# Pooled attention and a SiLU layer: one more seven-product unit in two tiles, weight sums one tile earlier, and two PSUM banks swapped

## The chip, the cores and the metric

The kernel runs on one core of a Trainium2 chip. The metric is the device time of one execution in microseconds; lower is better. Before the change three runs gave 282.60, 282.61 and 282.72 us, the median is 282.61.

## What is computed

Two stages in a row. The first is attention with keys and values that are averaged over groups of 8 positions (8 batches, 8 heads, 576 positions, 64 elements a head, so 72 pooled keys). The second multiplies the 4608 resulting rows of 512 by `w_in` (512 x 2048), applies SiLU, and multiplies by `w_out` (2048 x 512).

```python
k_p = k.reshape(B, H, Sp, pool, D).mean(axis=3)
v_p = v.reshape(B, H, Sp, pool, D).mean(axis=3)
scores = scale * np.matmul(q, k_p.transpose(0, 1, 3, 2))
attn = np.exp(scores - np.max(scores, axis=-1, keepdims=True))
attn = attn / (np.sum(attn, axis=-1, keepdims=True) + 1e-09)
x = np.matmul(attn, v_p)            # then transposed to rows of 8 * 64
h = x @ w_in
g = h * (1.0 / (1.0 + np.exp(-h)))
out = g @ w_out
```

## The kernel before

**Tiles.** The 4608 rows are taken in nine tiles of 512 (the loop over `t` at L793). Each tile has a first product (`up`, L460: `x` times `w_in`, SiLU into `h_T`) and a second product (`down` L562 in tile 0, `down_quarters` L632 in the others). The attention of batch `t + 1` is worked into the steps of tile `t`. Its results go into `xT`, a ring that holds the rows of four batches.

**Order.** Nothing is scheduled by the compiler: each engine runs its instructions in the order in which the Python code emits them. `spread` (L406) mixes two streams. A step of the product is two or four matmuls of `up`, or one of `down`; before it goes on past step `i`, it emits every "filler" that is due at `i` or earlier. `f_up` and `f_down` are the lists of fillers of a tile's two products, pairs of a due step and a function. So the due step sets the place in each engine's queue, and it sets nothing else: an instruction on DVE starts when the ones ahead of it on DVE are done and its own data are there.

**Units.** The 2048 columns of `w_in` are 16 groups of 128. A plain group (`plain`, L527) is four matmuls of 512 columns. Four groups can be computed as a "unit" (`UNITS` L417: groups 4 to 7, 8 to 11, 12 to 15): a two-by-two block scheme with seven products in place of eight (the Winograd form of Strassen's scheme). Its products are numbered 2, 5, 1, 4, 3, 7, 6 (`stage`, L491); each is four matmuls of 256 columns into one of three PSUM banks P, Q and R (L477). ScalarE copies P (`r_sb`, L494), DVE forms `rr_sb` (L497), `t_sb` (L500) and two sums `c_sb` (L509, L512), and ScalarE takes SiLU of P, Q and of the two sums (L485, the letters `h` and `s`). A unit needs five sums of parts of `x` (`unit_x_sum`, L442) and five sums of parts of `w_in` (`unit_weight_sum`, L435). In the lists at L807 to L821, `G(12)` is a plain group, `(0, "251")` are three products of unit 0; in `THREE` (L786) the letters A, B, C name units 0, 1, 2 (`"BCA".index` maps them to numbers), `g` a plain group. Before the change tile 1 has one unit and twelve plain groups, tile 2 two units and eight, tiles 3 to 8 three units and four.

**The second product.** From tile 1 on it uses the same scheme with seven products over sums of `h_T` (`hidden_sum`, L602) and five sums of quarters of `w_out` (`weight_sum`, L620). Each of these is emitted in four DVE instructions of 128 x 512. In `W_SUMS` (L612), `W11` and `W12` are rows 0 to 7 (of 16 groups of rows) of the left and right half of `w_out`, `W21` and `W22` rows 8 to 15. Sums 1 and 3 are emitted in tile 0's second product (steps 48 and 52), sums 4, 7 and 6 in tile 1's first product (steps 38, 42 and 60), at L834.

**Loads around it.** All loads from L706 on stand in POOL's queue in the order of the code. `w_out` comes in four quarters of four row groups (`load_w_out`, L729): quarters 0, 1 and 2 (L775), then three loads of the values of batch 1 (L777 to L779), then quarter 3 (L780). In tile 0's second product DVE pools these values (`slot_sums("v", j)`, due at steps 20 and 30, L849), PE selects the pooled rows (`select_v`, L294, steps 37 and 40), DVE copies them (`copy_v`, L308), and the attention of batch 1 is finished (`numerators`, L371, steps 44, 55 and 56), whose DVE products (L393) write the `xT` that tile 1 reads.

**Banks.** PSUM's eight banks are two rings: "mm" with three banks, "at" with five (L89). A new tile takes the oldest bank of its ring, and its first writer waits until the last reader of that bank is done. In the prologue (L736 to L769) `numerators(0, part(1, 0), ("mm", "at"))` puts its first product in an "mm" bank and its second in an "at" bank; the scores that follow take four "at" banks.

Of the kernel before, what the change touches and what calls it, by code (L numbers as in the profile page):

```python
# [36 lines left out]
def kernel(  # L37
# [11 lines left out]
    B, H, S, D = q.shape  # L49
# [148 lines left out]
    def pool_k(b):  # L198
        pool_rows(kp[:SP], batches[b]["k_raw"])
# [91 lines left out]
    def copy_k(b, a, copy=nc.vector.tensor_copy):  # L291
        copy(out=kz[b % 2][:, a], in_=batches[b]["kz_ps"][:, a])
# [21 lines left out]
    def part(g, f):  # L314
        return ((g, f * QF, (f + 1) * QF),)
# [302 lines left out]
    PW = 4  # L618
# [73 lines left out]
    def warm_up(n):  # L692
        for _ in range(n):
            nc.tensor.matmul(warm_ps, lhsT=warm[:, :128], rhs=warm, start=True, stop=True)  # L694
# [70 lines left out]
    scores(0, part(0, 1))  # L765
    q_transpose(0, 1, 1)
    warm_up(1)
    numerators(0, part(1, 0), ("mm", "at"))
    scores(0, part(1, 1))  # L769
    load_slots(nc.gpsimd, 1, "k", 0, 3)  # L770
    load_slots(nc.gpsimd, 1, "k", 3, 4)
# [21 lines left out]
    for t in range(NT):  # L793
        a = t + 1
        f_up, f_down = [], []
        if t == 0:
            GA = 11
            items = [(g, 0, HS) for g in range(GA)]
            items += [(g, HS, NTT - HS) for g in range(GA)]
            items += [(g, 0, NTT) for g in range(GA, KG)]  # L800
            f_up += [(1, lambda: denominators(0, part(0, 1), on_dve=True))]
            f_up += [(5, lambda: denominators(0, part(1, 1), on_dve=True))]
            f_up += [(13, lambda: numerators(0, part(0, 1)))]
            f_up += [(17, lambda: numerators(0, part(1, 1)))]
        else:
            G = lambda *gs: [(g, 0, NTT) for g in gs]
            if t == 1:  # L807
                items = (
                    G(12, 13, 14, 15) + [(0, "251")] + G(8) + [(0, "43")] + G(9)
                    + [(0, "7h6")] + G(10) + [(0, "s")] + G(11, 0, 1, 2, 3)  # L810
                )
            elif t > 2:
                items = []
                for it in THREE[t // B].split():
                    items += [(("BCA".index(it[0])), it[1])] if it[0] in "ABC" else G(int(it[1]))
            else:
                items = (
                    G(12, 13) + [(0, "251")] + G(14) + [(0, "43")] + G(15) + [(0, "76")]
                    + [(1, "2")] + [(0, "hs")] + [(1, "51")] + G(0) + [(1, "43")] + G(1)
                    + [(1, "7h6")] + G(2) + [(1, "s")] + G(3)  # L820
                )  # L821
            if t < 3:
                for n in U_X:
                    f_up.append((0, lambda n=n: unit_x_sum(t, n)))
            for n in (2, 5):
                h_at = 50 if t == B else 54 if t > 2 else 45
                f_up.append((h_at, lambda n=n: hidden_sum(n, 4, 8)))
            f_up.append((56, lambda: hidden_sum(6, 4, 8)))
            for n, k0 in ((2, 0), (5, 0), (1, 4), (1, 0)):
                f_up.append((64, lambda n=n, k0=k0: hidden_sum(n, k0, k0 + 4)))  # L830
            f_down.append((33, lambda: hidden_sum(7, 0, 8)))
            f_down.append((71 if t < B else 50, lambda: hidden_sum(6, 0, 4)))

        for n, t0, f_to, at, parts in (  # L834
            (1, 0, f_down, 48, (0, PW)), (3, 0, f_down, 52, (0, PW)),
            (4, 1, f_up, 38, (0, PW)), (7, 1, f_up, 42, (0, PW)),
            (6, 1, f_up, 60, (0, PW)),
        ):
            for i in range(*parts):
                if t == t0:  # L840
                    f_to.append((at + i, lambda n=n, i=i: weight_sum(n, i)))
        if a < B:
            q_at = [4, 14, 4, 8] if t > 2 else [15, 16, 17, 8] if t > 1 else [24, 25, 26, 2] if t else [82, 84, 86, 88]
            if t == 0:
                for j in range(2):
                    f_up.append((44 + 8 * j, lambda j=j: slot_sums("k", j)))
                    f_up.append((72 + 8 * j, lambda j=j: select_k(1, j)))
                    f_up.append((72 + 8 * j, lambda j=j: copy_k(1, j)))
                    f_down.append((20 + 10 * j, lambda j=j: slot_sums("v", j)))  # L849
                    f_down.append((37 + 3 * j, lambda j=j: select_v(1, j, "at")))  # L850
                    f_down.append((37 + 3 * j, lambda j=j: copy_v(1, j)))
            elif t == 1:
                for j in range(2):
                    f_up.append((0, lambda j=j: slot_sums("k", j, halves=True)))
                    f_up.append((22, lambda j=j: select_k(2, j)))
                    f_up.append((23, lambda j=j: copy_k(2, j)))
                    f_down.append((8, lambda j=j: slot_sums("v", j, halves=True)))
                    f_down.append((40, lambda j=j: select_v(2, j, "at")))
                    f_down.append((41, lambda j=j: copy_v(2, j)))
            else:  # L860
                f_up.append((1, behind_x_sums))
                f_up.append((1, lambda: pool_k(a)))
                if a + 1 < B:
                    f_up.append((2, lambda: load_one(a + 1, "k")))
                f_up.append((2, lambda: pool_v(a)))
                f_up.append((40, lambda: k_transpose(a)))
            for n in range(4):
                f_to = f_down if t and n >= (2 if t > 2 else 3) else f_up
                f_to.append((q_at[n], lambda n=n: q_transpose(a, n % 2, n // 2)))
            if t == 0:  # L870
                f_down.append((0, lambda: load_half_2("k", 0)))
                f_down.append((0, lambda: load_q(2)))
                f_down.append((0, lambda: load_half_2("k", 1)))
                for half in range(2):
                    f_down.append((31, lambda half=half: load_half_2("v", half)))
                for y in range(2):
                    for n in U_W:
                        f_down.append((6, lambda y=y, n=n: unit_weight_sum(y, n)))
            elif a + 1 < B:
                if t == 1:  # L880
                    f_up.append((0, lambda: load_one(a + 1, "k")))
                f_to, at = (f_up, 4) if t > 1 else (f_down, 11)
                f_up.append((5 if a + 1 == B - 1 else 0, lambda: load_q(a + 1)))
                f_to.append((at, lambda: load_one(a + 1, "v")))
                f_up.append((5, lambda: load_rest(a + 1, "k")))
                f_to.append((at + 2, lambda: load_rest(a + 1, "v")))
            f_down.append((0, attn_tables))

            if t:
                sc_at, den_at, nu_at = (1, 31, 75), (31, 56, 97), (56, 97, 101)  # L890
            else:
                sc_at, den_at, nu_at = (1, 16, 30), (16, 30, 44), (44, 55, 56)
            for n, sg in enumerate(visits):
                f_down.append((den_at[n], lambda sg=sg: denominators(a, sg)))
                f_down.append((sc_at[n], lambda sg=sg: scores(a, sg)))

            for n, sg in enumerate(visits):
                if n < 2 or not 0 < t < B - 2:
                    f_down.append((nu_at[n], lambda sg=sg: numerators(a, sg)))
                if n == 0 and 1 < t < B - 1:  # L900
                    f_down.append((nu_at[n], lambda: numerators(a - 1, visits[2])))
        if 1 < t < B:
            for n in (4, 1, 3, 7, 6):
                f_down.append((98 if t < B - 1 else 44, lambda n=n: unit_x_sum(t + 1, n)))
        if t == 1:
            def unit_weight_tiles():
                k_w = big.tile([128, 4, 2, 256], BF16, tag="k_raw2", name="w_sum12")
                v_w = big.tile([128, 4, 2, 256], BF16, tag="v_raw2", name="w_sum12")
                w_sum1.append([k_w[:, i] for i in range(4)] + [v_w[:, 0]])

            f_down.append((72, unit_weight_tiles))
            for i, n in enumerate(U_W):
                f_down.append((73 if i < 2 else 81, lambda n=n: unit_weight_sum(2, n)))
        moe_tables()
        up(t, f_up, items)
        if t == 0:
            down(t, f_down, [(0, 1, 2), (3,)])
        else:
            down_quarters(t, f_down, last=t == NT - 1)
# [28 lines left out]
```

The softmax here doesn't subtract the row's maximum and nothing guards it: scores larger than these inputs give would overflow.

## Time and profile before

| | us |
|---|---|
| median of three runs | 282.61 |
| the profiled execution | 282.59 |
| its span in the profile | 280.5 |
| busy PE / DVE / ACT / POOL | 275.4 / 218.2 / 187.7 / 98.7 |
| tile 0's second product begins | 32.84 |
| tile 1, 2, 3, 4 begin | 51.11, 81.35, 111.62, 140.35 |
| tile 1's, tile 2's second product begins | 65.18, 94.50 |

The span is the time from the first to the last instruction; the execution's own time has 2.09 us around it. All times of single instructions are microseconds from the span's start. In a timeline a line gives the start, the time until the last of the group ends, engine, source line, operation, what is written from what, and how many; in square brackets stand the idle time ahead of it and what ended it. PE is TensorE, PEld its weight loads, DVE VectorE, ACT ScalarE, POOL GpSimd, SP SyncE. The profile's ends of matmuls are modelled, so starts are what is compared here.

### The profile page before, as it was taken

Reading aid. Unit: us, or ns where it says so; the run is one execution under the profiler, and the core shown is the slowest. Engines: PE = TensorE matmul, PEld = TensorE weight load, DVE = VectorE, ACT = ScalarE, POOL = GpSimd, SP = SyncE. Lnnn points to the kernel's source line nnn. Section 1 sums busy time; section 2 is a strip of 40 time slices with the busy share of each in tenths; the row PEclk is TensorE's granted clock in tenths of the full one; section 3 lists DMA queues with packets and bytes.
Section 4 is the critical chain, followed back from the end, with each engine's and each line's share of the span. In section 5 each row is a group of like instructions: output and inputs, shape, how many; then the busy total and the mean of one; then the engine's idle time right before and its main releaser. Section 6 shows DMA issues by size and latency. Waiting matters only on the chain.

```text
span 280.5 us, 7088 instructions
## 1 busy us (share of the span) xinstructions
PE 275.4 (98%) x2853; PEld 201.4 (72%) x2853; DVE 218.2 (78%) x409; ACT 187.7 (67%) x365; POOL 98.7 (35%) x104
## 2 busy tenths in 40 slices
PE   8999999999999999999999999999999999999995
PEld 4448444556777578867888878787877778788684
DVE  4886746889887876897689768885888588966983
ACT  1688765668677776797579857984799578326700
POOL 8745217332138630863077106970640000000001
PEclk9999999999999999999999999999999999999999
DMA  7999999795659769569755944699610041004104
GB/s 210 284 260 238 210 325 171 227 197 94 148 72 203 200 108 170 129 181 132 138 132 154 135 65 121 141 144 139 160 26 2 0 105 49 0 11 109 33 4 148
DMA packets 31312, 37.70 MB, mean 134 GB/s; under 512 B 10352, under 2 KB 22256, under 8 KB 31280
## 3 DMA queue, kind: packets, MB, share of 16 engines
q0 software_dynamic: 23920, 27.03, 51.7%
q1 hardware_dynamic: 6928, 9.58, 12.4%
q10 hardware_dynamic: 432, 0.66, 0.6%
q8 instruction: 22, 0.36, 0.5%
q14 instruction: 10, 0.08, 0.1%
HBM read 36.70 MB, written 9.44 MB: 164 GB/s over the span
## 4 chain that ended last, share of the span: by engine, by line
PE 82%; DMA 12%; DVE 3%; issue 1%; ACT 1%; DVEq 0%
PE o_psP L645 15%; PE o_psQ L645 15%; PE hp_ps L537 13%; PE u_psP L477 10%; PE u_psQ L477 10%; PE o_psR L645 5%; DMA w_out_sb<-in_moe_w_out_dram 5%; DMA raw<-in_k_dram 4%; DMA q_bf<-in_q_dram 3%; PE u_psR L477 3%; PE sc_ps L340 3%; PE nu_ps L384 2%; PE warm_ps L694 2%; PE den_ps L358 2%; PE warm_ps L698 1%
## 5 line engine op out<-in xcount | busy, mean ns | idle before, releaser
L645 PEld LDWEIGHTS <-h_sum 128*128 128x128 bf16 x640 | 60.4, 98 | 13.1 <-DVE h_sum L605 2.7
L537 PE MATMUL hp_ps<-xT,w_in_sb 128*128 128x512 bf16 (+3 forms) x300 | 58.1, 337 | 0.1
L605 DVE TENSOR_TENSOR h_sum<-h_T 128x1024 bf16<-128x1024 bf16 (+1 forms) x72 | 51.9, 771 | 1.0 <-ACT h_T L543 1.0
L477 PEld LDWEIGHTS <-w_sum 128*128 128x128 bf16 x420 | 41.1, 98 | 7.7
L543 ACT ACTIVATE h_T<-hp_ps 128x512 bf16<-128x512 f32 (+2 forms) x71 | 36.3, 528 | 12.9 <-PE hp_ps L537 11.7
L348 ACT ACTIVATE es<-sc_ps 72x384 bf16<-72x384 f32 (+1 forms) x100 | 39.1, 470 | 8.8 <-PE sc_ps L340 8.7
L537 PEld LDWEIGHTS <-w_in_sb 128*128 128x128 bf16 x300 | 28.6, 98 | 18.4 <-issue 1.1
L485 ACT ACTIVATE h_T<-c_sb 128x512 bf16<-128x512 f32 x42 | 26.1, 627 | 4.9 <-DVE c_sb L509 4.3
L393 DVE TENSOR_TENSOR xT<-nu_ps,rec 128x384 bf16<-128x384 f32 (+1 forms) x50 | 24.0, 532 | 4.3 <-PE nu_ps L384 4.3
L645 PEld LDWEIGHTS <-h_T 128*128 128x128 bf16 x256 | 24.1, 98 | 4.5 <-issue 0.9
L549 POOL DMA_DIRECT2D out_dram<-o_sb x2 | 1.2, 618 | 68.3 <-issue 67.6
L367 ACT ACTIVATE lnd<-den_ps 128x384 f32<-128x384 f32 (+1 forms) x23 | 11.1, 484 | 19.7 <-PE den_ps L358 19.7
L190 POOL TENSOR_TENSOR raw<-raw 72x1024 f32<-72x1024 f32 x10 | 23.6, 2360 | 0.1
L500 DVE TENSOR_TENSOR t_sb<-u_psR,rr_sb 128x512 f32<-128x512 f32 x21 | 14.5, 692 | 6.7 <-PE u_psR L477 4.8
L494 ACT COPY r_sb<-u_psP 128x512 f32<-128x512 f32 x21 | 12.3, 584 | 10.1 <-PE u_psP L477 8.7
L263 DVE TENSOR_TENSOR raw<-raw 128x384 f32<-128x384 f32 (+3 forms) x20 | 12.4, 618 | 8.5 <-DMA raw<-in_v_dram 4.9
L645 PE MATMUL o_psP<-w_out_sb,h_sum 128*128 128x256 bf16 x128 | 17.7, 273 | 0.6 <-DVE h_sum L605 0.6
L477 PEld LDWEIGHTS <-w_in_sb 128*128 128x128 bf16 x168 | 16.1, 98 | 2.6
L497 DVE TENSOR_TENSOR rr_sb<-u_psQ,r_sb 128x512 f32<-128x512 f32 x21 | 14.3, 681 | 3.7 <-ACT r_sb L494 2.1
L509 DVE TENSOR_TENSOR c_sb<-u_psP,t_sb 128x512 f32<-128x512 f32 x21 | 14.4, 687 | 3.1 <-ACT h_T L485 1.4
L196 POOL COPY gate<-x_sum 1x1 bf16<-1x1 bf16 x5 | 0.9, 180 | 44.9 <-DVE x_sum L444 44.9
L645 PE MATMUL o_psQ<-w_sum,h_sum 128*128 128x256 bf16 x128 | 16.7, 273 | 0.0
(84 smaller groups left out, 518.6 us busy)
## 6 DMA issues: line engine op xcount, KB each, us to landing
out_dram<-o_sb SPq DMA_DIRECT2D x128, 64.0 KB, 1.8
raw<-in_k_dram POOLq DMA_DIRECT2D x10, 576.0 KB, 8.1
raw<-in_v_dram POOLq DMA_DIRECT2D x10, 576.0 KB, 7.8
q_bf<-in_q_dram POOLq DMA_DIRECT2D x6, 576.0 KB, 10.9
w_in_sb<-in_moe_w_in_dram POOLq DMA_DIRECT2D x8, 256.0 KB, 8.5
w_out_sb<-in_moe_w_out_dram POOLq DMA_DIRECT2D x4, 512.0 KB, 13.2
raw<-in_v_dram POOLq DMA_DIRECT2D x2, 768.0 KB, 11.0
raw<-in_k_dram POOLq DMA_DIRECT2D x1, 768.0 KB, 10.7
```

Source lines behind the costliest of these rows:

```text
L190: nc.gpsimd.tensor_add(out=raw[:, :, : 2 * D], in0=raw[:, :, : 2 * D], in1=raw[:, :, 2 * D :])
L348: nc.scalar.activation(es[:, s, :], sc[s], func=AF.Exp, scale=score_scale)
L393: nc.vector.tensor_mul(out=xT[:, 2 * g0 + c : 2 * (g0 + ng - 1) + c + 1 : 2, cols], in0=nu[c][:, :w].rearrange("r (g n) -> r g n", g=ng), ...
L477: nc.tensor.matmul(ps[y, bank][:, u, :], lhsT=w[:, kk, 128 * u : 128 * (u + 1)], rhs=x[:, kk, :], start=first and u == 0 and kk == 0, stop ...
L485: nc.scalar.activation(h_T[:, g : g + 2, j * NQ : (j + 1) * NQ], src, func=AF.Silu)
L497: tt(out=rr_sb, in0=ps[y, "Q"], in1=r_sb, op=ALU.add)
L500: tt(out=t_sb, in0=ps[y, "R"], in1=rr_sb, op=ALU.subtract)
L509: tt(out=c_sb[0], in0=ps[y, "P"], in1=t_sb, op=ALU.add)
L537: nc.tensor.matmul(hp_ps[:, r0:r1], lhsT=w_in_sb[:, kk, g * 128 : (g + 1) * 128], rhs=xT[:, kk, x0 : x0 + r1 - r0], start=(kk == 0), stop= ...
L543: nc.scalar.activation(h_T[:, g, n0 : n0 + n], hp_ps[:, :n], func=AF.Silu)
L605: nc.vector.tensor_tensor(out=h_sum[n][:, ks, :], in0=quarter(*a, ks), in1=quarter(*b, ks), op=op)
L645: nc.tensor.matmul(ps[b][:, c, :], lhsT=left(n, kt, c), rhs=W_OUT[n][:, kt, :], start=b not in begun, stop=kt == k1 - 1, skip_group_check= ...
```

## The change

Five edits in the Python code, all of order and place:

- Tile 2 takes the list `THREE` and the due steps of tiles 3 to 7: three units and four plain groups, hidden sums at step 54, query transposes at steps 4 and 14 of the first and 4 and 8 of the second product.
- Tile 1 takes a list with two units and eight plain groups, close to the one that tile 2 had. In it products "4 3" follow "2 5 1" without a plain group between.
- The sums of `x` for tile 2's units are emitted at the end of tile 1's second product, not at the start of tile 2.
- Weight sums 6, 4 and 7 (twelve DVE instructions, in that order) are emitted in tile 0's second product, due at steps 8, 12 and 16, not in tile 1's first product.
- In the prologue the second product of `numerators(0, part(1, 0))` takes an "mm" bank.

```diff
-    numerators(0, part(1, 0), ("mm", "at"))
+    numerators(0, part(1, 0), ("mm", "mm"))
...
             if t == 1:
                 items = (
-                    G(12, 13, 14, 15) + [(0, "251")] + G(8) + [(0, "43")] + G(9)
-                    + [(0, "7h6")] + G(10) + [(0, "s")] + G(11, 0, 1, 2, 3)
+                    G(12, 13, 14, 15) + [(0, "251")] + [(0, "43")] + G(0) + [(0, "76")]
+                    + [(1, "2")] + [(0, "hs")] + [(1, "51")] + [(1, "43")] + G(1)
+                    + [(1, "7h6")] + G(2) + [(1, "s")] + G(3)
                 )
-            elif t > 2:
+            else:
                 items = []
                 for it in THREE[t // B].split():
                     items += [(("BCA".index(it[0])), it[1])] if it[0] in "ABC" else G(int(it[1]))
-            else:
-                items = (
-                    G(12, 13) + [(0, "251")] + G(14) + [(0, "43")] + G(15) + [(0, "76")]
-                    + [(1, "2")] + [(0, "hs")] + [(1, "51")] + G(0) + [(1, "43")] + G(1)
-                    + [(1, "7h6")] + G(2) + [(1, "s")] + G(3)
-                )
-            if t < 3:
+            if t == 1:
                 for n in U_X:
                     f_up.append((0, lambda n=n: unit_x_sum(t, n)))
             for n in (2, 5):
-                h_at = 50 if t == B else 54 if t > 2 else 45
+                h_at = 50 if t == B else 54 if t > 1 else 45
...
             (1, 0, f_down, 48, (0, PW)), (3, 0, f_down, 52, (0, PW)),
-            (4, 1, f_up, 38, (0, PW)), (7, 1, f_up, 42, (0, PW)),
-            (6, 1, f_up, 60, (0, PW)),
+            (6, 0, f_down, 8, (0, PW)), (4, 0, f_down, 12, (0, PW)),
+            (7, 0, f_down, 16, (0, PW)),
...
-            q_at = [4, 14, 4, 8] if t > 2 else [15, 16, 17, 8] if t > 1 else [24, 25, 26, 2] if t else [82, 84, 86, 88]
+            q_at = [4, 14, 4, 8] if t > 1 else [24, 25, 26, 2] if t else [82, 84, 86, 88]
...
-                f_to = f_down if t and n >= (2 if t > 2 else 3) else f_up
+                f_to = f_down if t and n >= (2 if t > 1 else 3) else f_up
...
-        if 1 < t < B:
+        if 0 < t < B:
             for n in (4, 1, 3, 7, 6):
                 f_down.append((98 if t < B - 1 else 44, lambda n=n: unit_x_sum(t + 1, n)))
```

## The prediction

> **What bounds the kernel now.** I read the page first, then the chain that ended last, then the timelines of PE, DVE and POOL from 10 to 170 us, and last the DMA view cut to single issues. The page's first part and the engine line of its chain:
>
> ```profile
> PE 275.4 (98%) x2853; PEld 201.4 (72%) x2853; DVE 218.2 (78%) x409; ACT 187.7 (67%) x365; POOL 98.7 (35%) x104
> PE 82%; DMA 12%; DVE 3%; issue 1%; ACT 1%; DVEq 0%
> ```
>
> PE is never long without work, so this kernel's time is PE's own work plus the few places where PE waits. An edit pays if it takes columns from PE or ends a wait; an edit off PE costs nothing until PE waits for it. So I price each part on PE's timeline, tile by tile.
>
> The tiles begin at 51.11 (tile 1), 81.35 (tile 2), 111.62 (tile 3) and 140.35 us (tile 4). Tile 2 lasts 30.27 us, tile 3 28.73. Part of the difference stands in the timeline of tile 2:
>
> ```profile
> 89.48 2.37 POOL L190 TENSOR_TENSOR raw<-raw 72x1024 f32<-72x1024 f32 x1
> 90.76 3.33 DVE L605 TENSOR_TENSOR h_sum<-h_T 128x1024 bf16<-128x1024 bf16 x2
> 91.94 1.60 POOL L193 TENSOR_TENSOR vp<-raw 72x512 bf16<-72x512 f32 x1
> 97.63 1.05 PE L645 MATMUL o_psP<-w_out_sb,h_sum 128*128 128x256 bf16 x8 [0.65 <-DVE h_sum L605]
> ```
>
> Two hidden sums that take 0.68 us each elsewhere take 1.66 and 1.75 beside POOL's additions, everything behind them on DVE comes late, and PE stands for 0.65 us.
>
> For the weight sums the second product of tile 0 matters (32.84 to 51.11 us). Its DVE and PE timelines:
>
> ```profile
> 30.59 3.40 DVE L437 TENSOR_TENSOR w_sum<-w_in_sb 128x512 bf16<-128x512 bf16 x10
> 38.89 1.55 DVE L263 TENSOR_TENSOR raw<-raw 128x768 f32<-128x768 f32 x2 [4.89 <-DMA raw<-in_v_dram]
> 41.92 0.29 DVE L267 TENSOR_TENSOR v<-raw 128x128 bf16<-128x128 f32 x1
> ...
> 46.87 2.76 DVE L623 TENSOR_TENSOR w_sum<-w_out_sb 128x512 bf16<-128x512 bf16 x8
> 49.55 1.94 DVE L393 TENSOR_TENSOR xT<-nu_ps,rec 128x384 bf16<-128x384 f32 x4
> ```
>
> ```profile
> 43.31 0.34 PE L303 MATMUL v_ps<-v,shifts 128*128 128x64 bf16 x6
> 43.49 0.81 PE L572 MATMUL o_ps<-w_out_sb,h_T 128*128 128x512 bf16 x3
> 44.16 0.34 PE L303 MATMUL v_ps<-v,shifts 128*128 128x64 bf16 x6
> 44.33 1.03 PE L572 MATMUL o_ps<-w_out_sb,h_T 128*128 128x512 bf16 x4
> ```
>
> DVE idles 4.89 us until the values of batch 1 land, adds them up (38.89 to 42.21), and 1.1 us later PE selects them. The loads stand in POOL's queue as w_out quarters 0, 1, 2, then the three value loads, then w_out quarter 3. POOL's timeline has the last issue, and the DMA view cut to it has its time to landing:
>
> ```profile
> 26.54 0.78 POOL L731 DMA_DIRECT2D w_out_sb<-in_moe_w_out_dram  x1 [0.58 <-DMA w_in_sb<-in_moe_w_in_dram]
> w_out_sb<-in_moe_w_out_dram POOLq DMA_DIRECT2D x1, 512.0 KB, 15.7
> ```
>
> So quarter 3 lands at 26.54 + 15.7 = 42.24. The first value load, issued at 24.08 with 14.8 to landing, gives 38.88, and DVE starts at 38.89: the sum can be trusted. The same view puts quarters 0, 1 and 2 at 31.6, 34.1 and 36.7.
>
> [...] four 512-column matmuls take 0.86, four 256-column ones 0.44. [...] the trace shows no DVE instruction passing another. [...] the trace has slow matmuls only at the start (nine warm-up ones in 4.02 us, later six in 1.47) and no long idle after. [...]
>
> **Part 1, units.** Four plain groups are 16 matmuls of 0.216 = 3.46 us; a unit is 28 of 0.109 = 3.05. Each added unit saves 0.40 on PE, so 0.81 in all.
>
> **Tile 2** gets tile 3's order: its queues are built the same, with the x sums (five, 1.76 us) moved to the end of tile 1, the hidden sums from step 45 to 54, two query transposes to the second product. In tile 3 POOL's additions end at 121.57 and the hidden sums start at 123.53, six at 0.68. So tile 2 should last 28.73: 30.27 − 28.73 = **1.54 off**, of which 0.40 is the unit and 1.14 are waits. Nothing is late next: in tile 3 PE runs without a break, and the third unit's weight sums already stood in tile 1 (done at 79.0).
>
> **Tile 1.** 0.40 from the unit. DVE loses 12 weight sums there; a wait for hidden sums near 68.6 (0.1) goes. Against it, products "2 5 1" are now followed by "4 3" without plain groups between. Product 4 needs ScalarE's copy of P: unit 0's was done at 56.06, and product 4 would start at 56.09. For unit 1 my count gives DVE's rr_sb 0.2 too late for product 3. I bound these waits, less the 0.1 that goes, between −0.1 and +0.8 (two scalar copies' worth of 0.4 beyond PE's own work); I take +0.1. **0.30 off.** Hidden sums stay at step 45 there, but POOL has no additions in tile 1, so tile 2's slow sums don't move there.
>
> **Part 2, weight sums.** 12 DVE instructions of 0.345 (8 took 2.76) move ahead of the value sums in DVE's program. Sum 6 needs quarters 0 and 1: it runs from 34.0 to 35.4, in the idle time. Sum 4 reads w_out rows 8 to 15; its first two parts wait for quarter 2 (36.7 to 37.4). Its third part reads quarter 3, and DVE waits to 42.24. Queued behind: five more sums, the value sums, copies of the pooled values, the x products. Six sums of 0.345 end at 44.31; the value sums (3.32 as before) at 47.63, the first half at 46.2. PE reaches the selection at 43.31, waits to 46.3, does three matmuls, and waits again to 47.75; the matmuls that began at 44.33 begin at 47.92. That is **3.59 added**. From there DVE and PE depend on each other as before (copies, x products, eight weight sums, x products), and tile 1 begins 3.59 later. The 4.3 us of DVE that tile 1 loses pay back only what is counted above. No DMA is moved; POOL's value loads for batch 2 wait for the value sums and slip about 2 us, ahead of sums that slip 3.6.
>
> Bounds: 0, if quarter 3 were there by the values' time; 3.59 plus a cold clock (below) above.
>
> **Part 3, prologue.** The second value product leaves the pool of five, so the next scores reuse older banks: they wait for exponentials 1 to 3 instead of 1 to 4 (ScalarE, 14.54 to 15.84, a quarter of which is 0.32). PE's scores there take 1.17 us, others 0.45. Gain 0 to 0.32. A loss is excluded: the bank it takes was read by the copy that this product needs anyway. I count **0**: DMA landings set the wait at 43.31, and PE would only wait longer.
>
> **Sum.** 3.59 − 1.54 − 0.30 = +1.75. The profiled execution took 282.59 (span 280.5 and 2.09 around it), 0.02 under the median of three, 282.61. 282.59 + 1.75 = **284.3**.
>
> **Rivals.** *Faster: the sums fit in DVE's idle time.* 12 sums are 4.14 us and the gap is 4.89, so they would fit if the data were there. Then 282.59 − 1.54 − 0.30 − 0.32 = 280.4. It decides at the landing of quarter 3: the delay on PE is landing − 38.65, so at 40.5 gains and loss are equal, and below that it is faster. Against it: the value loads ahead in the same queue land at 38.9 to 39.9, and the view says 42.24. 0.06.
>
> *The clock halves.* PE idles 3.0 us, up to 3.3 with the prologue's gain. [...] 286.2. 0.18.
>
> *Tile 1 crowds.* The bank waits of both units cost 1 us more than counted (P and Q are each read by ScalarE and DVE between two products): 285.3. 0.07.
>
> *Half of it.* A wait about half as long, near no change: 282.5. 0.03.
>
> The forecast itself has 0.66, with 283.5 to 285.1 as its own spread. About 0.2% (0.57 us) is what a measurement can tell from no change: faster 0.06, same 0.04, slower 0.90. The range reaches from 283.4 into the cold-clock case, 286.4.
>
> **What would show it.** Right: DVE idle of about 4.8 us before a weight sum of L623 that starts near 42.2, released by w_out's DMA; PE's selection (L303) near 46.3; tile 1 beginning near 54.7; tile 2 lasting 28.7 and its hidden sums at 0.68; tile 1 at 29.9. Wrong: weight sums done by 39 us; PE matmuls of 512 columns at over 0.4 us after 46 us; tile 1 over 30.5 us.

## The result, and the profile after

The changed kernel takes 285.41 us (median of six runs, 284.80 to 287.48) beside 282.61 for the kernel before (282.29 to 282.82): ratio 1.011, with a 95% interval from 1.0078 to 1.0142. It is slower, as forecast, by 1.1 us more than the 284.3 forecast, and it lies above the 283.5 to 285.1 that the forecast gave as its own spread. The profiled run took 285.45 us; its span is 283.6, that of before 280.5, so the trace has 3.1 us to explain.

The page of after, first the busy times and then the granted clock in 40 slices of 7.09 us:

```profile
PE 275.2 (97%) x2877; PEld 203.7 (72%) x2877; DVE 221.5 (78%) x417; ACT 188.5 (66%) x367; POOL 99.0 (35%) x104
PEclk9999998999999999999999999999999999999999
```

PE has 0.2 us less work by the record than before and yet the span is longer, so the loss is waiting or a lower clock, and not more work. The one 8 in the second line is the slice from 42.5 to 49.6 us, which is tile 0's second product.

DVE's timeline of after, in that product and, as last line, in tile 2:

```profile
36.79 0.76 DVE L623 TENSOR_TENSOR w_sum<-w_out_sb 128x512 bf16<-128x512 bf16 x2 [1.36 <-DMA w_out_sb<-in_moe_w_out_dram]
42.45 2.10 DVE L623 TENSOR_TENSOR w_sum<-w_out_sb 128x512 bf16<-128x512 bf16 x6 [4.90 <-DMA w_out_sb<-in_moe_w_out_dram]
44.47 1.54 DVE L263 TENSOR_TENSOR raw<-raw 128x768 f32<-128x768 f32 x2
...
47.71 0.41 DVE L310 CAST vp<-v_ps 72x256 bf16<-72x256 f32 x1
...
98.00 4.29 DVE L605 TENSOR_TENSOR h_sum<-h_T 128x1024 bf16<-128x1024 bf16 x7
```

PE's timeline of after, the two selections, what follows them, and the first unit products of tiles 2 and 3:

```profile
46.47 0.35 PE L303 MATMUL v_ps<-v,shifts 128*128 128x64 bf16 x6 [3.15 <-DVE v L267]
46.65 1.23 PE L572 MATMUL o_ps<-w_out_sb,h_T 128*128 128x512 bf16 x3
48.18 0.48 PE L303 MATMUL v_ps<-v,shifts 128*128 128x64 bf16 x6 [0.30 <-DVE vp L310]
48.47 1.90 PE L572 MATMUL o_ps<-w_out_sb,h_T 128*128 128x512 bf16 x4
...
86.10 0.60 PE L477 MATMUL u_psP<-xT,w_sum 128*128 128x256 bf16 x4
...
114.83 0.60 PE L477 MATMUL u_psP<-xT,w_sum 128*128 128x256 bf16 x4
```

The reader sees the forecast's wait in place: DVE idles 4.90 us in front of the sums, with the values of batch 1 already in SBUF (their last load landed at 40.1) behind them in its queue, and PE idles 3.15 us in front of the first selection. In tile 2 seven hidden sums take 4.29 us, where two took 3.33 before. The chain that ended last goes through the load and then through DVE (start, length, piece):

```profile
26.63 15.80 DMA w_out_sb<-in_moe_w_out_dram
...
42.45 2.10 DVE w_sum L623 x6
...
47.80 0.34 DVE vp L310
...
48.18 0.48 PE v_ps L303 x6
```

Two things in PE's lines were not forecast as they are. The second selection waits for `vp`, a copy, and not for the values; and four matmuls of 512 columns take 1.90 us, which took 1.03 before. The windows of after, cut where the clock changes (stretch; length and busy time of PE, PEld, DVE, ACT, POOL with the number of instructions; clock, DMA share, GB/s):

```profile
46.90:50.30 3.40, 3.10 (x14) 0.95 (x13) 1.90 (x6) 0.59 (x1) 1.86 (x3) 0.50 1.28 173
50.30:51.00 0.70, 0.70 (x22) 0.49 (x22) 0.43 (x2) 0.23 (x1) 0.00 (x0) 0.99 0.55 192
```

From 46.90 to 50.32 us the array has half its clock.

Where the 3.1 us come from, by the starts of the tiles:

| stretch | before | after | difference |
|---|---|---|---|
| start of tile 1 | 51.11 | 56.12 | +5.01 |
| tile 1 | 30.24 | 29.98 | −0.26 |
| tile 2 | 30.27 | 28.73 | −1.54 |
| sum | | | +3.21 |

The rest of the span is about 0.1 us shorter.

### The profile page after: what moved, and what is told of

It reads as the page before. It is cut to its first block, busy times and chain, and to the rows that moved or that the text cites. A ratio compares the mean times of both kernels' runs of the same rounds, so it can differ in the third digit from the quotient of the medians.

```text
span 283.6 us, 7154 instructions
## 1 busy us (share of the span) xinstructions
PE 275.2 (97%) x2877; PEld 203.7 (72%) x2877; DVE 221.5 (78%) x417; ACT 188.5 (66%) x367; POOL 99.0 (35%) x104
## 4 chain that ended last, share of the span: by engine, by line
PE 79%; DMA 12%; DVE 4%; POOL 2%; issue 1%; ACT 0%; DVEq 0%; ACTq 0%; POOLq 0%
PE o_psQ L645 15%; PE o_psP L645 15%; PE hp_ps L537 11%; PE u_psQ L477 11%; PE u_psP L477 11%; DMA w_in_sb<-in_moe_w_in_dram 6%; DMA w_out_sb<-in_moe_w_out_dram 6%; PE o_psR L645 5%; PE u_psR L477 3%; PE sc_ps L340 3%; PE nu_ps L384 2%; PE den_ps L358 2%; DVE w_sum L623 2%; DVE xT L393 1%; DVE raw L263 1%
## 5 line engine op out<-in xcount | busy, mean ns | idle before, releaser
L477 PEld LDWEIGHTS <-w_sum 128*128 128x128 bf16 x460 | 44.9, 98 | 8.3
L537 PE MATMUL hp_ps<-xT,w_in_sb 128*128 128x512 bf16 (+3 forms) x268 | 50.5, 332 | 0.1
L605 DVE TENSOR_TENSOR h_sum<-h_T 128x1024 bf16<-128x1024 bf16 (+1 forms) x72 | 49.7, 742 | 1.0 <-ACT h_T L543 1.0
L543 ACT ACTIVATE h_T<-hp_ps 128x512 bf16<-128x512 f32 (+2 forms) x63 | 31.4, 520 | 9.5 <-PE hp_ps L537 7.7
L537 PEld LDWEIGHTS <-w_in_sb 128*128 128x128 bf16 x268 | 25.5, 98 | 15.3 <-issue 1.1
L485 ACT ACTIVATE h_T<-c_sb 128x512 bf16<-128x512 f32 x46 | 28.6, 627 | 3.1 <-DVE c_sb L509 2.3
L500 DVE TENSOR_TENSOR t_sb<-u_psR,rr_sb 128x512 f32<-128x512 f32 x23 | 15.9, 692 | 6.9 <-PE u_psR L477 5.4
L477 PEld LDWEIGHTS <-w_in_sb 128*128 128x128 bf16 x184 | 17.6, 98 | 2.6 <-issue 0.3
L512 DVE TENSOR_TENSOR c_sb<-u_psQ,t_sb 128x512 f32<-128x512 f32 x23 | 15.8, 687 | 2.5 <-PE u_psQ L477 2.3
L509 DVE TENSOR_TENSOR c_sb<-u_psP,t_sb 128x512 f32<-128x512 f32 x23 | 15.8, 686 | 2.0 <-PE u_psP L477 1.0
L572 PE MATMUL o_ps<-w_out_sb,h_T 128*128 128x512 bf16 x64 | 16.6, 403 | 0.0
```

The lines of the kernel that those rows point to most:

```text
L477: nc.tensor.matmul(ps[y, bank][:, u, :], lhsT=w[:, kk, 128 * u : 128 * (u + 1)], rhs=x[:, kk, :], start=first and u == 0 and kk == 0, stop ...
L485: nc.scalar.activation(h_T[:, g : g + 2, j * NQ : (j + 1) * NQ], src, func=AF.Silu)
L500: tt(out=t_sb, in0=ps[y, "R"], in1=rr_sb, op=ALU.subtract)
L509: tt(out=c_sb[0], in0=ps[y, "P"], in1=t_sb, op=ALU.add)
L537: nc.tensor.matmul(hp_ps[:, r0:r1], lhsT=w_in_sb[:, kk, g * 128 : (g + 1) * 128], rhs=xT[:, kk, x0 : x0 + r1 - r0], start=(kk == 0), stop= ...
L543: nc.scalar.activation(h_T[:, g, n0 : n0 + n], hp_ps[:, :n], func=AF.Silu)
```

## The experiments

Each ratio is against runs of the kernel before on the same chip, whose median was 282.24, 282.34 or 282.12 us.

### The load alone: sums 4 and 7 without the late quarter

```diff
+        rd = slice(0, KQ // PW) if n in (4, 7) and i >= 2 else ks
-        nc.vector.tensor_tensor(out=W_OUT[n][:, ks], in0=a[:, ks], in1=b[:, ks], op=op)
+        nc.vector.tensor_tensor(out=W_OUT[n][:, ks], in0=a[:, rd], in1=b[:, rd], op=op)
```

The same twelve instructions at the same place, but the four that read quarter 3 read rows of an earlier quarter: half of two of the weight sums is computed from the wrong rows.

> The changed kernel in which the last two parts of weight sums 4 and 7 read the first rows of their quarter pairs in place of the last ones, so that no sum needs w_out's last quarter; the same 12 instructions in the same places, and part of the weights is computed from the wrong rows. Theory (the load, not DVE's work, makes the wait): the sums end by 39 us in DVE's idle time, no wait on PE, 280.4. Rival (12 sums ahead of the values are too much for DVE anyway): tile 1 begins over 1 us late, 282 or more.

Measured: 280.16 us (279.93 to 280.56), ratio 0.9922 [0.9911, 0.9934]. DVE's timeline:

```profile
36.77 2.77 DVE L624 TENSOR_TENSOR w_sum<-w_out_sb 128x512 bf16<-128x512 bf16 x8 [1.33 <-DMA w_out_sb<-in_moe_w_out_dram]
39.46 1.54 DVE L263 TENSOR_TENSOR raw<-raw 128x768 f32<-128x768 f32 x2
```

All sums are done by 39.5 us. PE selects at 42.99 without a wait, and tile 1 begins at 50.79. So DVE's 4.1 us of work do fit into its idle time; what makes the loss is the landing of one operand.

### The same load earlier in the queue

```diff
-    for c in range(3):
+    for c in range(4):
         load_w_out(c)
...
     load_slots(nc.gpsimd, 1, "v", 4, 5)
-    load_w_out(3)
```

> The changed kernel with w_out's last quarter issued ahead of the three value loads of batch 1 (two lines of POOL's queue exchanged). Theory (what decides is when the load of the last quarter lands): it lands near 39 and the values near 42, about 2.3 us later than now; DVE's sums end near 41, the value sums near 44.5, PE's second selection comes 1.2 us late and its clock stays whole: 280.2 plus 1.2, so 281.4. Rival (values late are as bad as sums late): 283 or more.

Measured: 281.60 us (281.42 to 281.67), ratio 0.9974 [0.9964, 0.9985]. DVE now waits for quarter 3 only until 39.46, and its value sums begin at 41.63. One line of DVE's timeline, then PE's:

```profile
39.46 2.10 DVE L623 TENSOR_TENSOR w_sum<-w_out_sb 128x512 bf16<-128x512 bf16 x6 [1.85 <-DMA w_out_sb<-in_moe_w_out_dram]
```

```profile
43.63 0.35 PE L303 MATMUL v_ps<-v,shifts 128*128 128x64 bf16 x6 [0.88 <-DVE v L267]
...
45.34 0.34 PE L303 MATMUL v_ps<-v,shifts 128*128 128x64 bf16 x6 [0.72 <-DVE vp L310]
```

Changing only the order of loads turns the loss into a small gain. It isn't the whole gain: six sums still stand between this landing and the value sums, to 41.56, and the first of the value loads, now behind quarter 3, lands at 41.56 too (issued at 24.76, 16.8 to landing). Two PE waits remain; tile 1 begins at 52.29, 1.18 later than before.

### The parts alone: tile 2, the sums, the prologue

Tile 2's part on the kernel before (the list `THREE`, its due steps and its x sums, nothing else; the lines with the due steps, as in the whole change, stand at the dots):

```diff
-            elif t > 2:
+            elif t > 1:
...
-        if 1 < t < B:
+        if 0 < t < B:
```

> The kernel before with tile 2's part alone: three units, the dues of tiles 3 to 7, its x sums in tile 1; tile 1 with one unit, weight sums in tile 1, banks as before. By the prediction's term for tile 2: 1.5 off, 282.3 less 1.5 is 280.8. Rival (part of the gain needs the emptier DVE of the changed tile 1): 281.5 or more.

Measured: 281.07 us (280.54 to 281.48), ratio 0.9954 [0.9941, 0.9966]. Tile 2 lasts 28.74 us, 1.53 less than before; the median falls by 1.27. The trace has a wait that before's has not:

```profile
PE o_ps L572 <- DMA w_out_sb<-in_moe_w_out_dram: 0.7, 1, 0.7
```

Here quarter 3, issued at 26.70, took 16.5 us and landed at 43.2, a microsecond later than in before's trace, with the same loads in the same order. PE itself then waits for it. The landing varies by about a microsecond between the profiled executions.

The weight sums alone on the kernel before:

```diff
-            (4, 1, f_up, 38, (0, PW)), (7, 1, f_up, 42, (0, PW)),
-            (6, 1, f_up, 60, (0, PW)),
+            (6, 0, f_down, 8, (0, PW)), (4, 0, f_down, 12, (0, PW)),
+            (7, 0, f_down, 16, (0, PW)),
```

> The kernel before with the weight sums moved into tile 0's second product and nothing else. By the changed kernel's trace: 3.9 us of wait and 1.0 us of half clock added, 0.1 off in tile 1: 287.1 with a granted clock near 0.994. Rival (units and sums together make the loss): under 285.5.

Measured: 287.49 us (286.99 to 288.12), ratio 1.0184 [1.0167, 1.0202]. The whole loss comes from this edit, and more: the other parts gain. Two of the four executions have a mean clock of 0.994 and took 286.99 and 287.01 us, as expected; the other two, the profiled one among them, have 0.988 and took 287.98 and 288.12. In the profiled one PE stands for 3.09 us, selects at 46.20, and tile 1 begins at 56.79. Tile 1 then lasts 29.99 us, with its one unit and twelve plain groups, 0.25 less than before. The windows:

```profile
44.00:45.26 1.26, 0.00 (x0) 0.00 (x0) 1.23 (x3) 0.00 (x0) 1.26 (x3) 1.00 0.66 124
45.26:52.10 6.84, 5.90 (x42) 2.51 (x43) 4.73 (x11) 1.60 (x3) 3.32 (x5) 0.50 1.02 197
```

The clock falls at 45.26, while PE is still idle, and stays at half for 6.84 us, twice the length that it has in after.

The prologue's bank alone on the kernel before:

```diff
-    numerators(0, part(1, 0), ("mm", "at"))
+    numerators(0, part(1, 0), ("mm", "mm"))
```

> The kernel before with the bank of the prologue's second value product changed and nothing else. The prediction bounds the gain at 0 to 0.3 us: with no wait for w_out's last quarter in the way it should show nearly whole, 282.3; if the load of w_out or the values sets tile 0, 282.6.

Measured: 282.30 us (281.92 to 283.37), ratio 1.0002 [0.9993, 1.0011]. On this chip the kernel before took 282.24, so this is no gain, though the number is the 282.3 of the first case; the interval leaves room for at most 0.2 us. The trace shows the eight scores of the prologue in 0.88 us in place of 1.17, and tile 1 begins at 50.86 in place of 51.11: in this execution the 0.3 us carry through, but the medians don't show them.

### The clock: PE kept busy through the wait

```diff
+                def keep_busy():
+                    busy_ps = ps_tile([128, 512], FP32, "at", "busy_ps")
+                    for _ in range(14):
+                        nc.tensor.matmul(
+                            busy_ps, lhsT=warm[:, :128], rhs=warm, start=True, stop=True
+                        )
+
+                f_down.append((37, keep_busy))
```

The changed kernel with fourteen matmuls ahead of the first selection, whose result nobody reads.

> The changed kernel with 14 matmuls on zeros ahead of PE's selection of the values in tile 0's second product (3.0 us of PE work in the wait of 3.15 us; their result is not used). Theory that the wait also halves PE's clock: the matmuls after it take 0.22 us from the start, tile 1 begins near 54.7 in place of 56.1, and the time falls by 1.2 to 1.6 from 285.4 to about 284.0, with less spread. Rival (the slow matmuls have another cause, or the wait alone makes the loss): no change, 285.4, or later by what the added matmuls overrun.

Measured: 284.57 us (284.36 to 285.07), ratio 1.0081 [1.0067, 1.0094]; the granted clock is 1.0 in all four executions, and in none of after's six. PE's timeline:

```profile
43.50 3.18 PE L843 MATMUL busy_ps<-warm 128*128 128x512 bf16 x14
47.06 0.35 PE L303 MATMUL v_ps<-v,shifts 128*128 128x64 bf16 x6 [0.38 <-DVE v L267]
...
48.78 0.34 PE L303 MATMUL v_ps<-v,shifts 128*128 128x64 bf16 x6 [0.72 <-DVE vp L310]
48.95 1.03 PE L572 MATMUL o_ps<-w_out_sb,h_T 128*128 128x512 bf16 x4
```

Useless work makes the kernel faster: 0.3% less than after by the ratios, though in this profile quarter 3 landed at 43.05, 0.6 later than in after's. The two intervals overlap, so the size rests on the traces (the table below). The 284.0 and the 54.7 that were expected did not come: tile 1 begins at 55.73 here, because of the later landing and because the half clock had cost only 0.99.

The same with four matmuls in place of fourteen:

```diff
-                    for _ in range(14):
+                    for _ in range(4):
```

> The kernel with 14 added matmuls ahead of the selection, with 4 in place of 14 (0.9 us in the wait, so that PE then stands still for some 2.3 us and not for 3.15). [...] granted clock 1.0 and 284.6 as with 14. If 2.1 us of standing still are enough [...] as the trace of the sums alone suggests (gap from 43.1, half clock from 45.3): below 1.0 in some or all executions, 285.2 to 287.

Measured: 286.45 us (285.83 to 287.30), ratio 1.0154 [1.0133, 1.0175]. PE waits 0.74 us for quarter 3 itself before the four matmuls, stands for 2.53 us before the first selection and 0.72 before the second, and then the clock falls (windows):

```profile
48.68:52.10 3.42, 3.42 (x31) 1.44 (x31) 1.49 (x3) 0.68 (x2) 1.01 (x2) 0.50 1.08 288
```

A shorter idle time did not keep the clock, and the half-speed stretch now lies wholly in work that PE could have done. Five traces and before's, by PE's starts (us):

| kernel | first selection | second, after the first | tile 1, after the second | half clock |
|---|---|---|---|---|
| before | 43.31 | 0.85 | 6.95 | none |
| w_out before the values | 43.63 | 1.71 | 6.95 | none |
| fourteen matmuls | 47.06 | 1.72 | 6.95 | none |
| after | 46.47 | 1.71 | 7.94 | 46.90 to 50.32 |
| four matmuls | 46.94 | 1.71 | 8.52 | 48.68 to 52.10 |
| sums only | 46.20 | 1.72 | 8.87 | 45.26 to 52.10 |

With the full clock the last stretch is 6.95 in each of the three traces. The half clock adds 0.99, 1.57 and 1.92 us, about half of the part of it that lies after the second selection (2.14, 3.42 and 4.18 us). Before the second selection it costs nothing: the second selection comes 1.71 or 1.72 us after the first at either clock, since DVE's copy sets it, and the slow matmuls only fill time in which PE would have waited.

### The sums left in tile 1

```diff
-            (6, 0, f_down, 8, (0, PW)), (4, 0, f_down, 12, (0, PW)),
-            (7, 0, f_down, 16, (0, PW)),
+            (4, 1, f_up, 38, (0, PW)), (7, 1, f_up, 42, (0, PW)),
+            (6, 1, f_up, 60, (0, PW)),
```

The changed kernel with the weight sums at their old place.

> The changed kernel with weight sums 4, 7 and 6 back where they were before (tile 1's first product); units and banks stay changed. Theory (the sums' wait for w_out's last quarter is the whole loss): no wait of DVE near 42, PE selects the values near 43, tile 2 at 28.7, and 282.6 less 1.5 (tile 2), 0.3 (tile 1) and 0.3 (prologue): 280.5. Rival (the denser tile 1 or the lost plain groups cost it): still over 284. A third case, the sums crowd DVE in the new tile 1: 281 to 282.

Measured: 282.32 us (281.99 to 282.92), ratio 1.0002 [0.9994, 1.001]. The 280.5 that my theory gave was wrong, and the third case, that the sums crowd DVE, came, a little above its 281 to 282. Tile 2 lasts 28.73 us here too, but tile 1 lasts 32.07 in place of 29.98. DVE's timeline of tile 1:

```profile
66.91 1.43 DVE L623 TENSOR_TENSOR w_sum<-w_out_sb 128x512 bf16<-128x512 bf16 x4
68.25 2.49 DVE L605 TENSOR_TENSOR h_sum<-h_T 128x1024 bf16<-128x1024 bf16 x4
```

and PE's:

```profile
65.85 0.49 PE L340 MATMUL sc_ps<-qT,kz 32*72 32x192 bf16 x13 [0.60 <-DVE c_sb L509]
...
68.99 1.05 PE L645 MATMUL o_psP<-w_out_sb,h_sum 128*128 128x256 bf16 x8 [0.96 <-DVE h_sum L605]
```

With a second unit, DVE has no room for twelve weight sums in tile 1: they push back the unit's `c_sb` and the hidden sums that the second product begins with. The first product takes 13.98 us in both kernels; from the start of the second product to its second group of `o_psP`, the last line above, it is 4.33 in place of 2.32, which is 2.01 of the 2.09. So the parts can't be priced one by one: two units in tile 1 need the sums elsewhere. Little is won with the second unit, though: with the sums moved, tile 1 lasts 29.99 us with one unit (the sums alone) and 29.98 with two.

### The sums at the time of their data

```diff
-            (6, 0, f_down, 8, (0, PW)), (4, 0, f_down, 12, (0, PW)),
-            (7, 0, f_down, 16, (0, PW)),
+            (6, 0, f_down, 8, (0, PW)), (4, 0, f_down, 12, (0, 2)),
+            (7, 0, f_down, 14, (0, 2)), (4, 1, f_up, 1, (2, PW)),
+            (7, 1, f_up, 2, (2, PW)),
```

The eight instructions whose operands are there early stay in tile 0; the four that read quarter 3 go to the start of tile 1.

> The changed kernel with the sums divided by the quarter that they read: sum 6 and the first two parts of 4 and 7 at steps 8 to 15 of tile 0's second product (8 instructions, in DVE's idle time before the values), the last two parts of 4 and 7 at the start of tile 1 behind the key sums (4 instructions, 1.4 us). Nothing is left out. Theory: no wait, whole clock, tile 1 near its 30.0: 280.2, under the kernel before by 2. Rival (the four instructions in tile 1 delay rr_sb and with it the unit): 280.7 to 281.5.

Measured: 280.04 us (279.88 to 280.27), ratio 0.9918 [0.9905, 0.9932], faster than both kernels. DVE's timeline:

```profile
36.74 1.43 DVE L623 TENSOR_TENSOR w_sum<-w_out_sb 128x512 bf16<-128x512 bf16 x4 [1.35 <-DMA w_out_sb<-in_moe_w_out_dram]
39.04 1.55 DVE L263 TENSOR_TENSOR raw<-raw 128x768 f32<-128x768 f32 x2 [0.87 <-DMA raw<-in_v_dram]
...
54.54 1.43 DVE L623 TENSOR_TENSOR w_sum<-w_out_sb 128x512 bf16<-128x512 bf16 x4
```

DVE is idle again in front of the value sums, for 0.87 us and for the values' own landing. PE has no wait after its warm-up, the clock is 1.0, tile 1 begins at 50.93 and lasts 29.98, tile 2 lasts 28.73. The same with the prologue's old bank:

```diff
-    numerators(0, part(1, 0), ("mm", "mm"))
+    numerators(0, part(1, 0), ("mm", "at"))
```

> The kernel with the divided sums (280.0), with the prologue's second value product back in its old bank. If the bank is worth what the traces show at the start of tile 0 (0.3 us): 280.3. If it is worth nothing once the loads set tile 0's pace: 280.0.

Measured: 280.08 us (280.01 to 280.58), ratio 0.9924 [0.9911, 0.9938], which can't be told from 0.9918. In the two traces tile 1 begins at 51.25 with the old bank and 50.93 with the new one, so there the 0.3 us carry through, as they did on the kernel before. The medians don't show them: the bank is worth nothing that the times measure, and why the traces differ from them is open.

## Why the prediction was right, and 1.1 us short

**Direction and mechanism.** Right. DVE stops at the sum that reads quarter 3, everything queued behind it stops too, and PE waits for the values. It is shown from three sides: without the read of quarter 3 the loss is gone, with the four late instructions elsewhere it is gone, and with the load earlier PE waits 1.60 us in place of 3.45 and the kernel is faster than before. The signs that the prediction named came: DVE idle for 4.90 us until 42.45, PE's selection at 46.47, tile 2 at 28.73 and tile 1 at 29.98.

**Tile 2, −1.54.** Measured −1.54 in after and −1.53 alone. The forecast took tile 3's duration, because tile 2 got tile 3's order; this was better than adding up instructions. The hidden sums follow each other at some 0.6 us again (seven in 4.29, from 98.00 on), behind POOL's additions, which end at 96.53; in before the two beside the additions took 1.66 and 1.75. That the additions slow the sums is read from these two traces and was not tested apart. How the 1.54 divides among the third unit, the order and the later hidden sums was not measured.

**Tile 1, −0.30.** Measured −0.26, from parts that nearly cancel. For unit 1 the prediction counted `rr_sb` 0.2 us too late for product 3, and after's trace has this wait:

```profile
65.46 0.69 DVE L497 TENSOR_TENSOR rr_sb<-u_psQ,r_sb 128x512 f32<-128x512 f32 x1 [0.18 <-ACT r_sb L494]
65.48 0.60 PE L477 MATMUL u_psP<-x_sum,w_in_sb 128*128 128x256 bf16 x4
66.20 0.60 PE L477 MATMUL u_psQ<-x_sum,w_in_sb 128*128 128x256 bf16 x4
```

Product 3 (`u_psQ`) starts 0.72 us after product 4 (`u_psP`), where such products follow each other at 0.44: some 0.28 us are lost. `rr_sb`, which reads the bank that product 3 writes, ends at 66.15 (65.46 and 0.69), just ahead of it. The wait takes back most of the 0.40 that the unit saves, so the first product is only 0.09 shorter than before (13.98 for 14.07). The other 0.17 comes from the second product (16.00 for 16.17), and the sums alone, without the second unit, have it too (15.99). Whether the kernel with divided sums would be as fast with one unit in tile 1 was not run.

The rival "tile 1 crowds" did not come in this kernel. With the sums left in tile 1 a crowded tile came (+1.83 against before), but through DVE's queue and not through the banks that the rival named. The prediction did not see it: of the DVE time freed there I wrote "pay back only what is counted above", and without that time tile 1 with two units lasts 2.09 us longer.

**Weight sums, +3.59.** Measured +5.01. The terms, by the starts that the prediction gave:

| step | forecast | measured | added to the error |
|---|---|---|---|
| first selection | 46.3 | 46.47 | 0.17 |
| second, after the first | 1.45 | 1.71 | 0.26 |
| tile 1, after the second | 6.95 | 7.94 | 0.99 |
| tile 1 begins | 54.70 | 56.12 | 1.42 |

The first term is the landing: 26.63 + 15.80 = 42.43 where I had 42.24. The second is a queue that I read only in part: the second selection waits for the copy of the first half (L310), and this copy stands in DVE's queue behind the second half's value sums, so 0.3 us of it is added to the values' own time. In before DVE had time to spare and the copy was hidden. It is in the code's order (steps 30, 37 and 40) and could have been counted. In the execution's time the 1.42 show as 1.1, because the rest of the span is 0.1 us shorter and the time around the span was 0.24 shorter than the 2.09 that the forecast added.

The third is the clock, and there a step failed: I took a gap of 3.0 us, up to 3.3, to be too short for the clock to fall, which no trace of before showed, and gave the rival 0.18. The prediction's own sign of being wrong came, matmuls of 512 columns at over 0.4 us after 46 (four in 1.90, from 48.47). The clock fell after a gap of 3.15 us, in the sums alone 2.15 us into a gap, and with four matmuls after gaps of 2.53 and 0.72 with work between. The rival's price of 1.9 (286.2 − 284.3), my estimate with no trace behind it, was too high for this kernel: 1.28 us of the half-clock stretch lay before the second selection, which DVE sets, and only 0.99 was paid. So the forecast's mechanism and the rival's came together, and the time lies between their 284.3 and 286.2: inside the stated range because the range was stretched to take in the rival.

That the profiled run is no chance case shows in the others: five of the six runs of after have a granted clock of 0.993 or 0.994. Estimated from these means, that is 3.4 us at half clock (0.006 × 283.6 / 0.5), as in the profiled run; the longest, 287.48 us, has 0.988, by the same estimate 6.9 us (0.012 × 285.6 / 0.5). With the sums alone and with four matmuls, too, the executions at 0.988 are the long ones, by about 1.1 us in the mean.

**Prologue, 0.** Right for the changed kernel, in which PE waits for the values anyway. Where it doesn't wait, two pairs of traces carry 0.25 and 0.32 us on to tile 1, and the times don't show them.

**The faster rival, 280.4.** It named nearly the right time for the case that the data were there: 280.16 with other rows, 280.04 with the split. This is in part luck, since its sum has 0.32 for the prologue, which the times don't show. Its turning point, a landing at 40.5, is not refuted by the load moved ahead, which DVE had at 39.46 and which gained 0.26%; but tile 1 was delayed by 1.18 us there and not by 39.46 − 38.65 = 0.81; 0.26 of the difference is the copy again.

**What stays open.** How long PE may idle before the clock falls, and why it stayed down for 6.84 us with the sums alone where it stayed down for 3.42 in after, these runs don't settle. In the first half of the 6.84 us PE was idle for 0.94; in after's 3.42 it was idle for 0.30 and in that of the four matmuls not at all, and there the clock came back. Whether the copy could come before the second half's value sums was not tried.

## What to carry to other kernels

Before an instruction is moved into the idle time of an engine, look up when each of its operands lands, part by part: here one operand that landed at 42.43 held DVE for 4.90 us, and with it everything behind in DVE's queue, and splitting the instruction group by landing time kept the whole gain (280.04 us). Price an added wait on PE with what it does to the clock as well as its length: here the half clock added 0.99 to 1.92 us. Where one edit frees an engine for another, measure the two together as well as apart.

## What the runs showed of the hardware that was not expected

- The half clock lasted 3.42 us (after, four matmuls) or 6.84 us (sums alone). It fell 0.43 us after a gap of 3.15 had ended (after), 2.15 us into a gap of 3.09 (sums alone) and, with four matmuls, 0.03 us after the end of a gap of 0.72, which followed one of 2.53 with 0.99 us of work between. Gaps of 0.88 and 0.72, also with 0.99 between (w_out before the values), left the clock at 1.0, and so did gaps of 0.53, 0.38 and 0.72 (fourteen matmuls). These runs show no limit sharper than that.
- The same load, 512 KB in the same place of its queue, landed between 42.1 and 43.2 us in different traces; before's 42.24 was at the early end. In the three traces in which it landed at 42.9 or later, PE waited for it directly, 0.5 to 0.7 us.
- The time around the span was 2.09 us in before's profiled run and 1.85 in after's (285.45 − 283.6), so spans and times of single runs agree only to about 0.2 us.
